# Softmax weight sums moved from TensorE, ScalarE and VectorE to DMA transposes and GpSimd, in a fused attention and ReGLU kernel

## The chip, the core and the metric

The kernel runs on one core of one Trainium2 chip. The metric is the device time of one launch, in microseconds (us), as the median of several runs. Each run also lists the core's span (first to last instruction) and its mean granted TensorE clock, 1.0 being full speed (in the trace of before, an output matmul of 512 columns has a record of 0.39 us at 1.0 and of 0.61 us at 0.5). Engines: TensorE (PE; its weight loads are PEld), VectorE (DVE), ScalarE (ACT), GpSimd (POOL), SyncE (SP), which issues the DMAs. In the code, PSUM is the memory that the matmuls write, handed out in banks ("gate banks" for the gates, one "output bank"); all other tiles on the chip lie in SBUF.

## The reference

Two attention steps through 32 inducing points, then a gated feed-forward layer.

```
x: 4 x 12416 x 128      inducing: 32 x 128      scale = 1/sqrt(128)
mab(q, kv): a = softmax(scale * q @ kv.T);  return a @ kv
h   = mab(inducing, x)            # 4 x 32 x 128
y   = mab(x, h)                   # 4 x 12416 x 128, flattened to 49664 rows
out = (relu(y @ w_gate) * (y @ w_val)) @ w_out      # d_ff = 1536, fp32 out
```

Each row's softmax weights have to be divided by their sum. Gate and value are both linear in the weights, and ReLU passes a positive factor through, so the kernel leaves the 32 weights p2 of a row undivided and multiplies the output row twice by 1/sum at the end. The sum itself ("weight sum", z2) is what the change moves.

## The kernel before

x of one batch is cut into 24 blocks of 512 rows and a rest of 128. Since `y @ w_gate` is `p2 @ (h @ w_gate)`, the kernel forms `hgv = h @ [w_gate | w_val]` once per batch, and gate and value come from matmuls with 32 contraction rows. A unit is one slice of 128 hidden columns for two blocks: four such matmuls, one ReLU of each gate bank on ScalarE, and one product gate x value on VectorE. There are 588 units in all, 147 a batch.

```
    # PSUM: "g" three banks (gates and everything small), "v" two double banks, "o" one bank
    def bank(tag, name, ...): bufs={"g": 3, "v": 2, "o": 1}[tag]
    ...
    # one slot of the loop: value matmuls of an older unit, gate matmuls of a new one,
    # perhaps one "fill" (small work that takes a gate bank), two or so steps of an output chain
        g16 <- Relu(gate banks)                     # ScalarE, two of 128x512
        dst <- g16 * v                              # VectorE, 128x1024
```

The weight sums, once for four blocks, as a fill:

```
    def ev_z2(b, qd, first, last):
        def pe(at):
            ps = bank("g", "z2_ps", [P, TPB, 4])
            for t in range(TPB):
                nc.tensor.matmul(ps[:, t, :], p2qs[(b, qd)][:, cols], sel4, ...)
            ...
            def act():  nc.scalar.copy(out=z2, in_=ps)
            def dve():  nc.vector.reciprocal(out=z2i, in_=z2)
```

The weights of four blocks come out of one Exp as p2q (four row groups of 32); eight DMAs of 32 rows copy them twice each, because in this kernel the gate and the value matmuls of a unit read different rows (in the trace of before two gate and two value matmuls then start together, at 655.12 and 655.13 us):

```
        for j in range(2):
            for k in range(2):
                for d in range(2):
                    nc.sync.dma_start(
                        out=p2[j][64 * k + 32 * d : 64 * k + 32 * d + 32, :],
                        in_=p2q[64 * j + 32 * k : 64 * j + 32 * k + 32, :])
```

While a batch is worked on, h of the next one is collected in parts. The "join" adds the parts with small fp32 matmuls (two calls, four records in the trace); where it comes, near the end of a batch, is called the hand-over. It takes the only output bank, in the queue of output chains:

```
        def join():
            ps = s["hz_ps"] = bank("o", "hz_ps", [P, 2, M], FP32)
            nc.tensor.matmul(ps[:, 0, :], s["hp"][:, 0:P], stackI, ...)
            nc.tensor.matmul(ps[:, 1, :], s["zl"], stackI, ...)
        ...
        s["join"] = ([(at0 + 124, join)], finish, ([1], [1]))     # finish: VectorE makes hT
```

The softmax here doesn't subtract the row's maximum and nothing guards it: scores larger than these inputs give would overflow.

Of the kernel before, what the change touches and what calls it, by code (L numbers as in the profile page):

```python
# [10 lines left out]
FP32 = mybir.dt.float32  # L11
# [7 lines left out]
def kernel(  # L19
# [85 lines left out]
    sel2 = constp.tile([P, 2], FP16, name="sel2")  # L105
    nc.vector.memset(sel2, 0.0)
    nc.vector.memset(sel2[0:32, 0:1], 1.0)
    nc.vector.memset(sel2[64:96, 1:2], 1.0)
    sel4 = constp.tile([P, 4], FP16, name="sel4")
    nc.vector.memset(sel4, 0.0)  # L110
    for r in range(4):
        nc.vector.memset(sel4[32 * r : 32 * r + 32, r : r + 1], 1.0)
# [45 lines left out]
    def hgv_pe(hT, k, ps=None):  # L158
        if ps is None:
            ps = bank("g", "hgv_ps")  # L160
        for r in range(4):
            nc.tensor.matmul(
                ps[32 * r : 32 * r + 32, :],
                hT[:, 0:M],
                (wg if r % 2 == 0 else wv)[:, k * BLK : (k + 1) * BLK],
                start=True,
                stop=True,
            )
# [9 lines left out]
    def s2_pair_pe(hT, xT, pr):  # L178
        ps = bank("g", "s2_ps")
        for k in range(2):  # L180
            nc.tensor.matmul(
                ps[64 * k : 64 * k + 64, :],
                hT,
                xTs(xT, (2 * pr + k) * TPB, TPB),
# [28 lines left out]
    def p2_copies(p2q):  # L213

        p2 = [st([P, BLK], FP16, "p2", 4) for _ in range(2)]
        for j in range(2):
            for k in range(2):
                for d in range(2):
                    nc.sync.dma_start(
                        out=p2[j][64 * k + 32 * d : 64 * k + 32 * d + 32, :],  # L220
                        in_=p2q[64 * j + 32 * k : 64 * j + 32 * k + 32, :],
                    )
        return p2

    def s2_rest_pe(hT, xT):
        ps = bank("g", "s2_ps")
        nc.tensor.matmul(ps[0:64, 0:P], hT, xTs(xT, NT - 1, 1), start=True, stop=True)
        return ps

    def s2_rest_exp(ps):  # L230
        p2 = st([64, P], FP16, "p2r", 2)
        nc.scalar.activation(out=p2, in_=ps[0:64, 0:P], func=AF.Exp, scale=sm_scale)
        return p2
# [150 lines left out]
    def ev_s2_pair(b, pr, first, last):  # L384
        def pe(at):
# [5 lines left out]
            post[at + 1].append(act)  # L391

        fill(first, last, pe)

    def ev_s2_quad(b, qd, first, last):
        def pe(at):
# [9 lines left out]
            post[at + 2].append(copies)  # L406

        fill(first, last, pe)

    def ev_s2_rest(b, first, last):  # L410
        def pe(at):
# [5 lines left out]
            post[at + 1].append(act)  # L417

# [3 lines left out]
    def ev_z2(b, qd, first, last):  # L422
        def pe(at):
            if qd < NPAIR // 2:
                ps = bank("g", "z2_ps", [P, TPB, 4])
                for t in range(TPB):
                    cols = slice(t * P, (t + 1) * P)
                    if (b, qd) in p2qs:
                        nc.tensor.matmul(
                            ps[:, t, :], p2qs[(b, qd)][:, cols], sel4, start=True, stop=True  # L430
                        )
                    else:
                        for j in range(2):
                            nc.tensor.matmul(
                                ps[:, t, 2 * j : 2 * j + 2],
                                p2s[(b, 2 * qd + j)][:, cols],
                                sel2,
                                start=True,
                                stop=True,
                            )  # L440
            else:
                ps = bank("g", "z2_ps", [P, 1, 1])
                nc.tensor.matmul(
                    ps[:, 0, :], p2s[(b, NPAIR)], sel2[0:64, 0:1], start=True, stop=True
                )

            def act():
                n = ps.shape[1] * ps.shape[2]
                tag = "4" if n > 1 else "1"
                z2 = st(ps.shape, FP32, "z2" + tag, 2)  # L450
                nc.scalar.copy(out=z2, in_=ps)

                def dve():
                    z2i = st(ps.shape, FP32, "z2i" + tag, 3)
# [526 lines left out]
```

## Time and profile before

| | before |
|---|---|
| median of the first three runs | 730.74 us (730.72 to 734.59) |
| VectorE busy | 95% |
| ScalarE busy | 94% |
| TensorE busy | 89% |
| GpSimd busy | 30% |
| granted clock, mean of the span | 0.991 |

Two engines run at their limit side by side. The lines themselves are shown in the prediction.

### The profile page before, as it was taken

What the parts mean: (1) busy time and instruction counts of PE and PEld (TensorE: products, weight loads), DVE (VectorE), ACT (ScalarE), POOL (GpSimd) and SP (SyncE); (2) the same over time, 40 slices, a digit from 0 to 9 for tenths busy, and PEclk for the clock granted to TensorE, in tenths of its full rate; (3) what the DMA queues carried; (4) which work ended last, traced back from release to release, by engine and by line L of the source; (5) the groups of instructions that cost most, each with busy time, mean ns of one, the idle gap of its engine ahead of it and who ended that gap; (6) DMA issues with size and microseconds to landing.
All of it is one profiled execution on the core that took longest, in us unless ns stands there. A gap on an engine that the chain in (4) does not pass through costs nothing.

```text
span 729.2 us, 14099 instructions
## 1 busy us (share of the span) xinstructions
PE 652.5 (89%) x4653; PEld 195.5 (27%) x4653; DVE 689.4 (95%) x666; ACT 682.9 (94%) x1400; POOL 220.5 (30%) x440
## 2 busy tenths in 40 slices
PE   5889898998898999898988999999889898898896
PEld 5422222222222222222222222222223222222222
DVE  4599999999999999999999999999999999999996
ACT  4599999998999999999999999999999999999985
POOL 3422325322131433433122243443212221221221
PEclk9999999999999999999999999999999999999999
DMA  9546667521256776722235975852212222222122
GB/s 339 200 115 166 146 160 167 109 74 51 57 135 137 189 173 154 175 75 72 44 76 152 152 200 127 197 121 74 65 55 77 58 80 63 61 80 66 59 66 71
DMA packets 130490, 84.57 MB, mean 116 GB/s; under 512 B 104912, under 2 KB 113904, under 8 KB 128112
## 3 DMA queue, kind: packets, MB, share of 16 engines
q1 hardware_dynamic: 130416, 83.67, 45.1%
q8 instruction: 36, 0.59, 0.4%
q14 instruction: 38, 0.31, 0.1%
HBM read 27.80 MB, written 25.43 MB: 73 GB/s over the span
## 4 chain that ended last, share of the span: by engine, by line
PE 40%; ACT 23%; issue 16%; DVE 15%; DMA 5%; SPq 1%; POOL 0%; ACTq 0%; DVEq 0%
PE o_ps L657 17%; ACT g L944 17%; DVE gv L947 14%; PE v_ps L849 12%; PE g_ps L849 6%; ACT oT L663 5%; DMA gv<-in_x_dram 2%; DMA out_dram<-osb 1%; PE s1T_ps L529 1%; PE idle_ps L278 1%; DMA p<-p2q 1%; PE s_ps L199 1%; PE o_ps L713 1%; ACT p2q L210 0%; ACT hgv L172 0%
## 5 line engine op out<-in xcount | busy, mean ns | idle before, releaser
L947 DVE TENSOR_TENSOR gv<-g,v_ps 128x1024 f16<-128x1024 f16 x576 | 662.8, 1219 | 17.0 <-PE g_ps L849 7.2
L944 ACT ACTIVATE g<-g_ps 128x512 f16<-128x512 f32 x1164 | 615.5, 616 | 24.4 <-PE g_ps L849 16.5
L657 PE MATMUL o_ps<-gv,wo 128*128 128x512 f16 x1128 | 340.8, 385 | 33.2 <-ACT oT L663 31.7
L849 PE MATMUL g_ps<-p,hgv 32*128 32x512 f16 x1152 | 285.9, 382 | 7.2 <-ACT g L944 2.3
L674 POOL TENSOR_SCALAR osb<-o,z2i 128x128 f32<-128x128 f16 x380 | 164.5, 447 | 404.3 <-DMA o<-oT 248.2
L849 PE MATMUL v_ps<-p,hgv 32*128 32x512 f16 x1152 | 227.6, 386 | 10.8 <-DVE gv L947 9.1
L849 PEld LDWEIGHTS <-hgv 32*128 32x128 f16 x2400 | 73.8, 91 | 269.1 <-issue 263.1
L657 PEld LDWEIGHTS <-wo 128*128 128x128 f16 x1176 | 79.3, 97 | 188.3 <-issue 162.1
L663 ACT CAST oT<-o_ps 128x512 f16<-128x512 f32 (+1 forms) x98 | 57.4, 586 | 0.1
L508 POOL CAST x<-x 128x2048 f16<-128x2048 f32 x18 | 34.0, 1890 | 16.6 <-DMA x<-in_x_dram 12.4
L613 POOL TENSOR_TENSOR hp<-hp,hq 128x129 f32<-128x129 f32 (+1 forms) x18 | 8.2, 456 | 48.6 <-ACT hq L612 43.6
L331 DVE COPY xT<-xT_ps 128x1024 f16<-128x1024 f16 (+1 forms) x13 | 8.5, 651 | 7.0 <-PE xT_ps L330 5.7
L210 ACT ACTIVATE p2q<-s_ps 128x512 f16<-128x512 f32 x23 | 14.0, 610 | 0.0
L302 ACT ACTIVATE p<-s_ps 128x256 f16<-128x256 f32 (+2 forms) x14 | 5.0, 356 | 7.6 <-PE s_ps L300 7.6
L539 ACT ACTIVATE p1T<-s1T_ps 128x512 f16<-128x512 f32 x18 | 11.9, 662 | 0.0
L330 PE MATMUL xT_ps<-eye,x 128*128 128x128 f16 x97 | 9.2, 249 | 1.6 <-POOL x L294 0.9
L294 POOL CAST x<-gv 128x1024 f16<-128x1024 f32 x6 | 6.2, 1040 | 12.6 <-DMA gv<-in_x_dram 12.6
L199 PE MATMUL s_ps<-xT,hT 128*32 128x512 f16 x92 | 9.2, 388 | 0.7
L292 ACT CAST x<-gv 128x1024 f16<-128x1024 f32 (+1 forms) x6 | 5.8, 967 | 3.9 <-DMA gv<-in_x_dram 3.9
L947 DVE TENSOR_TENSOR gvr<-g,v_ps 128x512 f16<-128x512 f16 x12 | 8.0, 684 | 1.5 <-PE g_ps L849 1.5
L529 PE MATMUL s1T_ps<-xT,indT 128*32 128x512 f16 x72 | 7.2, 388 | 1.1
L330 PEld LDWEIGHTS <-x 128*128 128x128 f16 x97 | 6.9, 112 | 2.3 <-POOL x L294 1.1
(101 smaller groups left out, 166.5 us busy)
## 6 DMA issues: line engine op xcount, KB each, us to landing
out_dram<-osb SPq DMA_DIRECT2D x94, 256.0 KB, 2.2
x<-in_x_dram SPq DMA_DIRECT2D x18, 1024.0 KB, 5.8
p<-p2q SPq DMA_DIRECT2D x184, 32.0 KB, 1.9
gv<-in_x_dram SPq DMA_DIRECT2D x11, 512.0 KB, 8.3
o<-oT SPq DMA_TRANSPOSE x98, 2.4
x<-in_moe_w_out_dram SPq DMA_DIRECT2D x1, 768.0 KB, 9.2
gv<-in_x_dram SPq DMA_DIRECT2D x2, 256.0 KB, 9.5
x<-in_moe_w_gate_dram SPq DMA_DIRECT2D x1, 512.0 KB, 8.0
```

Of the source, the lines that this page charges most:

```text
L199: nc.tensor.matmul(ps[32 * r : 32 * r + 32, :], hT[:, 0:M], xTs(xT, (4 * qd + r) * TPB, TPB), start=True, stop=True,)
L210: nc.scalar.activation(out=p2q, in_=ps, func=AF.Exp, scale=sm_scale)
L330: nc.tensor.transpose(ps[:, t - t0, :], x16[:, t, :], eye16)
L508: nc.gpsimd.tensor_copy(out=s["x16"][:, t0:t1, :], in_=s["x32", q])
L529: nc.tensor.matmul(ps[32 * r : 32 * r + 32, :], indT, xTs(s["xT"], t, TPB), start=True, stop=True,)
L539: nc.scalar.activation(out=p1T, in_=ps, func=AF.Exp, scale=sm_scale)
L657: nc.tensor.matmul(c["ps"][:, 0:w], wo[:, i, :], gv(i), start=(i == 0), stop=(i == NFF - 1))
L663: nc.scalar.copy(out=oT[:, 0:w], in_=c["ps"][:, 0:w])
L674: nc.gpsimd.tensor_scalar(out=osb[:, t, :], in0=o16[:, t, :], scalar1=zz, scalar2=zz, op0=ALU.mult, op1=ALU.mult,)
L849: nc.tensor.matmul(ps[:, cols], hgv[:, s * P : (s + 1) * P], p2, start=True, stop=True)
L944: nc.scalar.activation(out=g16[:, k * BLK : (k + 1) * BLK], in_=ps, func=AF.Relu)
L947: nc.vector.tensor_tensor(out=ready["dst"], in0=ready["g16"][:, 0:n], in1=ready["v"][:, 0:n], op=ALU.mult)
```

## The change

Its intent: take the weight sums off the three busy engines. p2q is transposed by DMA, so that a row's 32 weights lie along the free dimension; GpSimd adds them in five halvings and raises the sum to the power -1. Besides, the row order becomes gate, gate, value, value, so that two copies lie together and four DMAs of 64 rows do the work of eight; the join goes to the gate banks as a fill; three output rings (sets of buffers used in turn) get a fourth buffer.

```
-        for k in range(2):  for d in range(2):   # eight copies of 32 rows
+            for d in range(2):
+                nc.sync.dma_start(out=p2[j][64 * d : 64 * d + 64, :], in_=p2q[64 * j : 64 * j + 64, :])
... (rows of the matmul operands follow: gate 0 to 63, value 64 to 127)
-    def ev_z2(b, qd, first, last):          # matmuls, ScalarE copy, VectorE reciprocal
+    def ev_z2(p2, keys, n, at):
+        def tr():
+            nc.sync.dma_start_transpose(out=p2T, in_=p2()[0:rows, :])
+            def add():
+                m = M // 2
+                while m:
+                    nc.gpsimd.tensor_tensor(out=dst, in0=v[:, :, :, 0:m], in1=v[:, :, :, m:2*m], op=ALU.add)
+                    v, m = dst, m // 2
+                def power():
+                    nc.gpsimd.tensor_tensor(out=z2i, in0=v[:, :, :, 0], in1=minus1, op=ALU.pow)
+                post[at + 7].append(power)
+            post[at + 5].append(add)
+        post[at].append(tr)
...
-            ps = s["hz_ps"] = bank("o", "hz_ps", [P, 2, M], FP32)
+            ps = s["hz_ps"] = bank("g", "hz_ps", [P, 2, M], FP32)
-        s["join"] = ([(at0 + 124, join)], finish, ([1], [1]))
+        fill(at0 + 120, at0 + 124, join, True)
...
-            oT = st([P, BLK], FP16, "oT", 3)          # o16 and osb alike
+            oT = st([P, BLK], FP16, "oT", 4)
```

More of the change, by code (lines that the diff above doesn't have):

```diff
@@ L104 @@
     nc.vector.memset(ones16, 1.0)
-    sel2 = constp.tile([P, 2], FP16, name="sel2")
-    nc.vector.memset(sel2, 0.0)
-    nc.vector.memset(sel2[0:32, 0:1], 1.0)
-    nc.vector.memset(sel2[64:96, 1:2], 1.0)
-    sel4 = constp.tile([P, 4], FP16, name="sel4")
-    nc.vector.memset(sel4, 0.0)
-    for r in range(4):
-        nc.vector.memset(sel4[32 * r : 32 * r + 32, r : r + 1], 1.0)
+    minus1 = constp.tile([P, 4 * TPB], FP32, name="minus1")
+    nc.gpsimd.memset(minus1, -1.0)
     ind16 = constp.tile([M, C], FP16, name="ind16")
@@ L164, in hgv_pe @@
                 hT[:, 0:M],
-                (wg if r % 2 == 0 else wv)[:, k * BLK : (k + 1) * BLK],
+                (wg if r < 2 else wv)[:, k * BLK : (k + 1) * BLK],
                 start=True,
@@ L179, in s2_pair_pe @@
         ps = bank("g", "s2_ps")
-        for k in range(2):
+        for r in range(4):
             nc.tensor.matmul(
-                ps[64 * k : 64 * k + 64, :],
-                hT,
-                xTs(xT, (2 * pr + k) * TPB, TPB),
+                ps[32 * r : 32 * r + 32, :],
+                hT[:, 0:M],
+                xTs(xT, (2 * pr + r % 2) * TPB, TPB),
                 start=True,
@@ L216, in p2_copies @@
         for j in range(2):
-            for k in range(2):
-                for d in range(2):
-                    nc.sync.dma_start(
-                        out=p2[j][64 * k + 32 * d : 64 * k + 32 * d + 32, :],
-                        in_=p2q[64 * j + 32 * k : 64 * j + 32 * k + 32, :],
-                    )
+            for d in range(2):
+                nc.sync.dma_start(
+                    out=p2[j][64 * d : 64 * d + 64, :], in_=p2q[64 * j : 64 * j + 64, :]
+                )
         return p2
@@ L226, in s2_rest_pe @@
         ps = bank("g", "s2_ps")
-        nc.tensor.matmul(ps[0:64, 0:P], hT, xTs(xT, NT - 1, 1), start=True, stop=True)
+        for d in range(2):
+            nc.tensor.matmul(
+                ps[64 * d : 64 * d + 64, 0:P], hT, xTs(xT, NT - 1, 1), start=True, stop=True
+            )
         return ps
     def s2_rest_exp(ps):
-        p2 = st([64, P], FP16, "p2r", 2)
-        nc.scalar.activation(out=p2, in_=ps[0:64, 0:P], func=AF.Exp, scale=sm_scale)
+        p2 = st([P, P], FP16, "p2r", 2)
+        nc.scalar.activation(out=p2, in_=ps[:, 0:P], func=AF.Exp, scale=sm_scale)
         return p2
@@ L391, in pe @@
             post[at + 1].append(act)
+            ev_z2(lambda: p2s[(b, pr)], [(b, pr, k) for k in range(2)], TPB, at + 2)
         fill(first, last, pe)
@@ L406, in pe @@
             post[at + 2].append(copies)
+            keys = [(b, 2 * qd + j, k) for j in range(2) for k in range(2)]
+            ev_z2(lambda: p2qs[(b, qd)], keys, TPB, at + 7)
         fill(first, last, pe)
@@ L417, in pe @@
             post[at + 1].append(act)
+            ev_z2(lambda: p2s[(b, NPAIR)], [(b, NPAIR, 0)], 1, at + 3)
         fill(first, last, pe)
-    def ev_z2(b, qd, first, last):
-        def pe(at):
-            if qd < NPAIR // 2:
-                ps = bank("g", "z2_ps", [P, TPB, 4])
-                for t in range(TPB):
-                    cols = slice(t * P, (t + 1) * P)
-                    if (b, qd) in p2qs:
-                        nc.tensor.matmul(
-                            ps[:, t, :], p2qs[(b, qd)][:, cols], sel4, start=True, stop=True
-                        )
-                    else:
-                        for j in range(2):
-                            nc.tensor.matmul(
-                                ps[:, t, 2 * j : 2 * j + 2],
-                                p2s[(b, 2 * qd + j)][:, cols],
-                                sel2,
-                                start=True,
-                                stop=True,
-                            )
-            else:
-                ps = bank("g", "z2_ps", [P, 1, 1])
-                nc.tensor.matmul(
-                    ps[:, 0, :], p2s[(b, NPAIR)], sel2[0:64, 0:1], start=True, stop=True
-                )
-            def act():
-                n = ps.shape[1] * ps.shape[2]
-                tag = "4" if n > 1 else "1"
-                z2 = st(ps.shape, FP32, "z2" + tag, 2)
-                nc.scalar.copy(out=z2, in_=ps)
-                def dve():
-                    z2i = st(ps.shape, FP32, "z2i" + tag, 3)
-                    nc.vector.reciprocal(out=z2i, in_=z2)
-                    if n > 1:
-                        for j in range(2):
-                            z2is[(b, 2 * qd + j)] = z2i[:, :, 2 * j : 2 * j + 2]
-                    else:
-                        z2is[(b, NPAIR)] = z2i
-                post[at + 2].append(dve)
-            post[at + 1].append(act)
-        fill(first, last, pe, True)
@@ new lines, in ev_z2 @@
+    def ev_z2(p2, keys, n, at):
+        g = len(keys)
+        rows = P if g == 4 else 2 * M
+        def tr():
+            p2T = st([P, n, rows], FP16, "p2T%d" % g, 2)
+            nc.sync.dma_start_transpose(out=p2T, in_=p2()[0:rows, :])
+            def add():
+                v = p2T.rearrange("p n (g m) -> p n g m", m=M)[:, :, 0:g, :]
+                m = M // 2
+                while m:
+                    dst = st([P, n, g, m], FP32, "zt%d%d" % (g, m), 1)
+                    nc.gpsimd.tensor_tensor(
+                        out=dst, in0=v[:, :, :, 0:m], in1=v[:, :, :, m : 2 * m], op=ALU.add
+                    )
+                    v, m = dst, m // 2
+                def power():
+                    z2i = st([P, n, g], FP32, "z2i%d" % g, 3)
+                    nc.gpsimd.tensor_tensor(
+                        out=z2i,
+                        in0=v[:, :, :, 0],
+                        in1=minus1[:, 0 : n * g].rearrange("p (n g) -> p n g", n=n),
+                        op=ALU.pow,
+                    )
+                    for i, key in enumerate(keys):
+                        z2is[key] = z2i[:, :, i : i + 1]
+                post[at + 7].append(power)
+            post[at + 5].append(add)
+        post[at].append(tr)
@@ L484 @@
                 ev_s2_pair(b, 1, 5, 8)
-            ev_z2(b, qd, base + (0 if base else 10), base + (8 if base else 15))
+                ev_z2(lambda: p2s[(0, 0)], [(0, 0, k) for k in range(2)], TPB, 2)
         a = slot(b, NPAIR, 0)
         ev_s2_rest(b, a - 11, a - 4)
-        ev_z2(b, NPAIR // 2, a - 1, a + 6)
     def plan_phase1(b):
@@ L626, in h_part, with join @@
             post[at + 1].append(act)
-        def join():
-            ps = s["hz_ps"] = bank("o", "hz_ps", [P, 2, M], FP32)
+        def join(at):
+            ps = s["hz_ps"] = bank("g", "hz_ps", [P, 2, M], FP32)
             nc.tensor.matmul(ps[:, 0, :], s["hp"][:, 0:P], stackI, start=True, stop=True)
             nc.tensor.matmul(ps[:, 1, :], s["zl"], stackI, start=True, stop=True)
+            post[at + 1].append(lambda: finish(at + 1))
         def finish(at):
@@ L661, in evac @@
         def evac(at):
-            oT = st([P, BLK], FP16, "oT", 3)
+            oT = st([P, BLK], FP16, "oT", 4)
             nc.scalar.copy(out=oT[:, 0:w], in_=c["ps"][:, 0:w])
             def tr():
-                o16 = st([P, TPB, P], FP16, "o16", 3)
+                o16 = st([P, TPB, P], FP16, "o16", 4)
                 nc.sync.dma_start_transpose(out=o16[:, 0:nt, :], in_=oT[:, 0:w])
                 def scale():
-                    osb = st([P, TPB, P], FP32, "osb", 3)
-                    z = z2is[key]
+                    osb = st([P, TPB, P], FP32, "osb", 4)
+                    z = z2is[key + (k,)]
                     for t in range(nt):
-                        zz = z[:, t, k : k + 1]
+                        zz = z[:, t, :]
                         nc.gpsimd.tensor_scalar(
@@ L715, in evac @@
         def evac(at):
-            z = z2is[key][:, :, k]
+            z = z2is[key + (k,)][:, :, 0]
             zz = st([P, TPB], FP32, "zz", 2)
             nc.vector.tensor_tensor(out=zz, in0=z, in1=z, op=ALU.mult)
-            oT = st([P, BLK], FP16, "oT", 3)
-            osb = st([P, TPB, P], FP32, "osb", 3)
+            oT = st([P, BLK], FP16, "oT", 4)
+            osb = st([P, TPB, P], FP32, "osb", 4)
             for a in (0, h):
@@ L788, in units @@
                                 ]
-                                for r in (64 * k, 64 * k + 32)
+                                for r in (32 * k, 64 + 32 * k)
                             ],
@@ L807, in units @@
                         )
-                        if b + 1 < B and (pr, k) == (9, 0):
-                            job(*state[b + 1]["join"])
                     for s in range(NFF):
@@ L821, in units @@
                                     )
-                                    for k, r in ((0, 32 * j), (1, 64 + 32 * j))
+                                    for k, r in ((0, 64 * j), (1, 64 * j + 32))
                                 ]
@@ L842, in units @@
                                 ]
-                                for r in (0, 32)
+                                for r in (0, 64)
                             ],
```

## The prediction

> **What bounds the kernel now.** I read the page's busy shares first, then busy time by stretches, then VectorE's (DVE's) instructions in order of time. The first line is the busy share of each engine over the span. The other two are stretches of 100 us, with columns for busy time and instruction count of each engine, granted clock, DMA share and GB/s.
>
> ```profile
> PE 652.5 (89%) x4653; PEld 195.5 (27%) x4653; DVE 689.4 (95%) x666; ACT 682.9 (94%) x1400; POOL 220.5 (30%) x440
> ...
> 500.00:600.00 100.00, 89.34 (x602) 26.27 (x599) 97.84 (x93) 96.83 (x198) 24.49 (x57) 1.00 0.23 67
> 600.00:700.00 100.00, 88.84 (x556) 24.08 (x555) 100.00 (x93) 98.49 (x199) 25.64 (x60) 1.00 0.23 65
> ```
>
> The reader is to see two engines at their limit at once. In the last batch (600 to 700 us), which carries no preparation of a next batch, VectorE is busy 100.00 of 100 us, so every nanosecond taken from it shortens the run one for one. Before that VectorE idles about 2 us in 100 and ScalarE (ACT) 2 to 4, each waiting on the other through the gate banks. TensorE (89%) and GpSimd (POOL, 30%) have room. Now VectorE's timeline in the last batch: start, duration, instruction, count.
>
> ```profile
> 612.91 0.26 DVE L455 RECIPROCAL z2i<-z 128x16 f32<-128x16 f32 x1
> 613.07 27.19 DVE L947 TENSOR_TENSOR gv<-g,v_ps 128x1024 f16<-128x1024 f16 x24
> 640.15 0.27 DVE L455 RECIPROCAL z2i<-z 128x16 f32<-128x16 f32 x1
> 640.31 27.20 DVE L947 TENSOR_TENSOR gv<-g,v_ps 128x1024 f16<-128x1024 f16 x24
> ```
>
> Twenty-four products start between 613.07 and 640.15, so one costs 27.08 / 24 = 1.128 us of the engine. That is less than its own 1.219 us, because the next one starts before the last has ended. One reciprocal costs 613.07 - 612.91 = 0.16 us here, not the 0.25 us of its record. I price by starts, not durations, throughout.
>
> [...] between 60 and 716 us, 106 products that lie at least 80% beside GpSimd work average 1.217 us, and 289 beside none average 1.220. [...] The trace has 128x129 adds of 458 ns. [...] two gate and two value matmuls start within 0.01 us at 655.12 and 655.13.
>
> **The weight sums: removed.** For every four blocks there are four tiny matmuls, a ScalarE copy out of a gate bank and a VectorE reciprocal. The columns are count, then busy us and mean ns, then idle before:
>
> ```profile
> L429 PE MATMUL z_ps<-sel,p2q 128*128 128x4 f16 x92 | 5.5, 164 | 2.1
> L451 ACT COPY z<-z_ps 128x16 f32<-128x16 f32 x24 | 5.2, 217 | 0.0
> L455 DVE RECIPROCAL z2i<-z 128x16 f32<-128x16 f32 x24 | 6.0, 251 | 0.0
> ```
>
> With the four small ones of the rest blocks there are 28 each. VectorE: from each reciprocal's start to the next instruction's start the records sum to 6.6 us, of which 1.3 is idle that merely follows it; so 5.2 us is certain work and 6.6 the most. In the last batch they cost 0.155 us each. ScalarE: the 28 copies by the same count are 4.1 us (0.15 each), plus 0.5 idle after. TensorE: 92 + 8 + 4 matmuls, about 5.9 us, on an engine with room. The users of the third gate bank lose 28 members, which should ease some of the 7.2 us in which products waited for a gate matmul.
>
> **The weight sums: added.** 29 transposes by DMA (23 groups of four blocks, two pairs, four rests), and on GpSimd five adds and a power for each. The adds of a group make 256, 128, 64, 32 and 16 elements per partition. [...] GpSimd goes from 220 us to about 280 to 320, near 40%, still far from a bound.
>
> **The copies of p2.** SyncE issues them; each issue takes it 0.588 us (median of 184), 110.8 us in all. Half of them go: -55 us. The added transposes at 1.2 us an issue (median of the output transposes) are +33 us. These rows are count, KB each and median us to landing:
>
> ```profile
> p<-p2q SPq DMA_DIRECT2D x184, 32.0 KB, 1.9
> o<-oT SPq DMA_TRANSPOSE x98, 2.4
> ```
>
> Nothing on the compute engines waits for either now in any amount: p2q copies appear twice among the waits, 3.5 us together, on engines with slack. So this is worth about zero. The new row order puts the gate operands on rows 0 to 63 and the value operands on 64 to 127; the four matmuls still use four different row groups, so TensorE's time should not move.
>
> **The join.** Now it takes the only output bank, and the next output chain waits until VectorE has made hT:
>
> ```profile
> 176.09 0.35 DVE L148 RECIPROCAL rz<-hz_ps 128x32 f32<-128x32 f32 x1
> 176.48 0.23 DVE L150 TENSOR_TENSOR hT<-hz_ps,rz 128x64 f16<-128x64 f32 x1
> ...
> 176.76 0.61 PE L657 MATMUL o_ps<-gv,wo 128*128 128x512 f16 x1 [0.49 <-DVE hT L150]
> 177.30 0.11 PEld L849 LDWEIGHTS <-hgv 32*128 32x128 f16 x4 [0.44 <-issue]
> 177.31 0.61 PE L849 MATMUL v_ps<-p,hgv 32*128 32x512 f16 x2
> ...
> 177.30:180.40 3.10, 3.10 (x14) 0.63 (x13) 2.74 (x4) 1.99 (x4) 1.73 (x4) 0.56 0.19 73
> ```
>
> TensorE waits 0.49 us, and its clock falls to half: matmuls take 0.61 us instead of 0.39 and the granted clock (third from the end in the stretch line) is 0.56. The second hand-over (350 us) shows the same, the third (524 us) stays at 1.00. VectorE is busy 4.42, 4.53 and 4.96 us in the 5 us from 176, 350 and 524, so a slow stretch costs some 0.5 us there and, with the catching up after it, perhaps 0.9. Moving the join to the gate banks removes the wait; two joins give at most 1.8 us. But [...] VectorE's 0.5 us for hT now holds a gate bank. I count 0.8 us. The join may also come up to four slots earlier; its input zl was written 18.7 us before the join at 175.0, so it should not wait.
>
> **The sum.** Weight sums: between the 5.2 us certain and 6.6 us possible on VectorE, less something because ScalarE, which loses only 4.1 to 4.6 us, takes over as the limit before 600 us: 5.5 us. Join 0.8 us. Copies 0. From 730.7: 724.4 us, a ratio of 0.991.
>
> **Rivals.** *ScalarE becomes the bound.* It is within 1% of VectorE until 600 us and loses less; then the gain is some 4 us (727). For it: equal busy times. Against it: in the last batch only VectorE is full. *GpSimd or the transposes become a new wait*: [...] an add blocked behind a late transpose delays the scaling and the stores behind it, and after four output buffers ScalarE itself would stop. For it: transposes of x take 4.7 us to land and DMA is 0.6 to 0.7 busy in the loading stretches. Against it: each add comes five slots (some 5.7 us) after its transpose, each power seven after that, GpSimd now idles 70%, and the change deepens three output rings to four. If it bit, 733 to 745 us. *The gate banks gain more than I count*: 28 fewer users of the third bank could remove most of the small VectorE gaps, about 1 us in 50; then 719 to 721. *Nothing moves*, since the freed time turns into waits for the same gate matmuls: 729 to 731.
>
> **Range and chances.** The sum of small, mostly certain terms gives 724.4; the first and last rivals put the upper end at 729.5, the third the lower end at 719.5. Faster by over 2% would need 14.6 us, more than VectorE's removable work and half of its 17.8 us of idle between 30 and 722 us together: 0.02. Slower by over 2% needs the GpSimd rival to bite hard: 0.03. Within 2%: 0.95.
>
> **What would show it.** Right: in 600 to 700 us VectorE still full, with products at 1.128 us start to start and no reciprocals; ScalarE and VectorE busy about 4 and 6 us less; GpSimd near 300 us with no product slower than 1.22; SyncE's issue time down; no 0.49 us wait of TensorE at the hand-overs. Wrong: outputs' casts on ScalarE waiting for a transpose (a full ring), products longer beside GpSimd, power instructions of several us, gate and value matmuls no longer starting together, or the half clock appearing in new places.

The forecast's sum came to 5.5 + 0.8 + 0 = 6.3 us, that is 724.4 us. Terms are cut from the smaller sum, that of GpSimd's added work: what led to its total of 280 to 320 us came only in part from a trace, so that total stands as the author's estimate and no more. Of a slow stretch's "perhaps 0.9" us, the traces showed 0.43 to 0.54 beforehand (VectorE busy 4.42 and 4.53 us against 4.96); the rest of it, and the 0.8 us for the join, are the author's estimates too. Two readings in their numbers, from the waits of before: ScalarE's ReLUs waited 16.5 us and VectorE's products 7.2 us for gate matmuls; and one engine did wait for a DMA, GpSimd 248.2 us for output transposes, though it was busy only 30%.

## The result, and the profile after

The changed kernel takes 721.93 us (median of 4 runs, 721.80 to 723.25) against 730.86 us (4 runs): 8.9 us less, where I had said 6.3 less, and inside the range. The ratio is 0.987 with a 95% interval of 0.984 to 0.990; ratios here are the mean time of one kernel's fast runs over that of the other's of the same rounds, so not quite the ratio of the medians quoted. On a second chip it was 721.75 us against 733.16 us, 0.986 (0.983 to 0.988).

Page and stretches of the changed kernel, for the lines shown of before:

```profile
PE 640.5 (89%) x4557; PEld 190.3 (26%) x4557; DVE 685.1 (95%) x630; ACT 679.3 (94%) x1372; POOL 342.4 (48%) x615
...
500.00:600.00 100.00, 87.98 (x575) 25.57 (x574) 98.29 (x90) 97.48 (x195) 45.45 (x89) 1.00 0.25 72
600.00:700.00 100.00, 88.72 (x559) 24.01 (x556) 98.96 (x89) 97.33 (x193) 41.00 (x83) 1.00 0.25 72
```

VectorE and ScalarE are still the two full engines; VectorE's busy time fell by 4.3 us, ScalarE's by 3.6. GpSimd went up by 122 us. The small idle of VectorE in 600 to 700 is the last batch's rest, which now begins before 700. In VectorE's timeline from 600 to 660 us the reciprocals are gone, and 54 products run without a break:

```profile
599.76 61.17 DVE L934 TENSOR_TENSOR gv<-g,v_ps 128x1024 f16<-128x1024 f16 x54
```

The price on GpSimd, in its groups by shape (count, then busy us and mean ns, then idle before):

```profile
L442 POOL TENSOR_TENSOR z2i<-zt,minus 128x16 f32<-128x16 f32 x23 | 67.0, 2912 | 1.3
L435 POOL TENSOR_TENSOR zt<-p2T 128x256 f32<-128x256 f16 x23 | 15.3, 665 | 7.1 <-DMA p2T<-p2q 7.1
L435 POOL TENSOR_TENSOR zt<-zt 128x128 f32<-128x128 f32 x23 | 10.4, 453 | 1.8
L435 POOL TENSOR_TENSOR zt<-zt 128x64 f32<-128x64 f32 x25 | 8.0, 320 | 2.0
L435 POOL TENSOR_TENSOR zt<-zt 128x32 f32<-128x32 f32 x25 | 6.0, 241 | 2.0
L435 POOL TENSOR_TENSOR zt<-zt 128x16 f32<-128x16 f32 x25 | 5.4, 215 | 2.0
```

The five adds of a group take 665 + 453 + 320 + 241 + 215 = 1894 ns, the power of 16 elements 2.91 us (1.65 us for 8, 0.56 for 1). The products did not notice: some 210 of them beside GpSimd work average 1.213 us, 205 beside none 1.213.

The hand-over, now with the join in a gate bank (start, duration, engine, operation):

```profile
172.76 0.39 PE L619 MATMUL hz_ps<-stackI,zl 128*128 128x32 f32 x2
...
172.99 0.38 PE L646 MATMUL o_ps<-gv,wo 128*128 128x512 f16 x1
...
174.12 0.35 DVE L142 RECIPROCAL rz<-hz_ps 128x32 f32<-128x32 f32 x1
...
174.50 0.23 DVE L144 TENSOR_TENSOR hT<-hz_ps,rz 128x64 f16<-128x64 f32 x1
```

The next output chain starts at 172.99, right behind the join and 1.1 us before VectorE takes up h; no wait for hT is left. And the matmuls run at 0.38 us, the full clock.

**Where the clock was.** In these traces the stretches of half clock lie on a grid of 3.41 us: in that of before they begin at 29.86, 176.63 and 350.71 us, 43 and 51 times 3.413 us apart. These are two in the profile of before, each with the window ahead of it (columns as above; the third number from the end is the granted clock):

```profile
26.44:29.86 3.42, 2.18 (x21) 0.52 (x13) 2.05 (x4) 1.51 (x4) 1.98 (x2) 1.00 0.51 213
29.86:33.27 3.41, 3.41 (x14) 0.48 (x12) 2.98 (x3) 2.59 (x6) 1.38 (x1) 0.50 0.02 5
173.21:176.63 3.42, 2.67 (x22) 1.18 (x19) 3.39 (x6) 3.30 (x9) 0.68 (x2) 1.00 0.16 32
176.63:180.04 3.41, 3.28 (x13) 0.74 (x14) 3.05 (x5) 2.09 (x5) 1.73 (x4) 0.50 0.23 83
```

And the only one inside the loop of the changed kernel:

```profile
252.95:256.36 3.41, 2.60 (x18) 0.69 (x14) 3.41 (x4) 3.41 (x9) 1.09 (x3) 1.00 0.97 237
256.36:259.77 3.41, 3.41 (x15) 0.63 (x13) 2.60 (x3) 2.32 (x6) 0.00 (x0) 0.50 0.93 236
```

In a stretch TensorE is busy with hardly a pause (3.28 to 3.41 of 3.41 us), yet VectorE and ScalarE starve: in the last one VectorE works 2.60 of 3.41 us, ScalarE 2.32. In the window ahead of it TensorE had a lull: it was busy 2.18, 2.67 and 2.60 of 3.41 us. The prediction had seen two of these stretches (at the hand-overs), not the one at the start, and it priced the two as if they came in every run.

**Where the time went.** I lined up the starts of the 588 products of both kernels, in pieces in which neither profile has a half-clock stretch. Where one of the two had, I took the second profile of the same kernel (b_again, a_again, below). Starts in us from the span's start:

```
product     4      120     200     414     430     587
before    36.85  172.70  268.30  521.25  540.90  721.12
b_again   35.95  171.79  266.23  518.04  538.94  721.91
after     36.08  170.73  265.73  514.50  533.97  713.04
a_again   36.22  170.87  264.60  514.63  534.09  713.17

  4 to 120   before 135.85  after   134.65    1.20
120 to 200   b_again 94.44  a_again  93.73    0.71
200 to 414   b_again 251.81 after   248.77    3.04
414 to 430   before  19.65  after    19.47    0.18
430 to 587   before 180.22  after   179.07    1.15
                                       sum    6.28
```

So 6.3 us of the loop's gain has nothing to do with the clock. Another 1.0 us is the very end, from the end of the last product to the end of the span (6.9 us before, 5.9 after). The rest, 1.6 us of the 8.9, is left for fewer half-clock stretches. The same starts price a stretch: a piece that holds one is 1.1 to 1.4 us longer than the same piece without (seven cases in these four profiles, with starts of more products than the table has; 1.26 us on average).

### The profile page after: what moved, and what is told of

The parts are those of the page before. It is cut to its first block, busy times and chain, and to the rows that moved or that the text cites. A ratio compares the mean times of both kernels' runs of the same rounds, so it can differ in the third digit from the quotient of the medians.

```text
span 720.2 us, 13901 instructions
## 1 busy us (share of the span) xinstructions
PE 640.5 (89%) x4557; PEld 190.3 (26%) x4557; DVE 685.1 (95%) x630; ACT 679.3 (94%) x1372; POOL 342.4 (48%) x615
## 4 chain that ended last, share of the span: by engine, by line
PE 43%; ACT 22%; issue 16%; DVE 15%; DMA 4%; SPq 0%; POOL 0%; DVEq 0%; ACTq 0%
PE o_ps L646 19%; ACT g L931 15%; DVE gv L934 15%; PE v_ps L836 14%; PE g_ps L836 7%; ACT oT L652 6%; DMA gv<-in_x_dram 2%; PE s_ps L193 1%; DMA x<-in_x_dram 1%; PE o_ps L702 1%; PE s1T_ps L517 1%; PE idle_ps L273 0%; DMA p1r<-p1T 0%; ACT p1T L527 0%; ACT hgv L166 0%
## 5 line engine op out<-in xcount | busy, mean ns | idle before, releaser
L442 POOL TENSOR_TENSOR z2i<-zt,minus 128x16 f32<-128x16 f32 (+2 forms) x29 | 72.5, 2501 | 1.5
L435 POOL TENSOR_TENSOR zt<-zt 128x128 f32<-128x128 f32 (+5 forms) x116 | 33.4, 288 | 9.1
L435 POOL TENSOR_TENSOR zt<-p2T 128x256 f32<-128x256 f16 (+2 forms) x29 | 17.0, 586 | 12.5 <-DMA p2T<-p2q 7.1
```

Source lines behind the costliest of these rows:

```text
L435: nc.gpsimd.tensor_tensor(out=dst, in0=v[:, :, :, 0:m], in1=v[:, :, :, m : 2 * m], op=ALU.add)
L442: nc.gpsimd.tensor_tensor(out=z2i, in0=v[:, :, :, 0], in1=minus1[:, 0 : n * g].rearrange("p (n g) -> p n g", n=n), op=ALU.pow,)
```

## The experiments

Theory after the result: (a) the weight sums are worth 5 to 6 us because VectorE sets the pace; (b) the rest comes from half-clock stretches, which the join's place makes likelier, and from the fourth buffer at the end. Rivals: ScalarE sets the pace; the gate banks do; the clock is chance of chip and run; the added GpSimd and DMA work costs something that hides in the sum.

Names beginning with b change the kernel before, with a the changed kernel. "Stretches" are counted for each run from its mean granted clock g and span s, n = (1 - g) x s / 1.707 us (half of the 3.413 us that the stretches inside the loop take in the traces); g is given to 0.001, so n is good to about 0.2. A stretch after the last matmul counts too, with no matmul left to slow (in that of before from 726.17 us, the last matmul ending at 724.45): in the profiles it adds 0.8 to 1.0 to n in the kernel before and its variants, and 0 to 0.7 in the changed kernel and its variants. So about 2.7 of the 3.5 before and 0.8 of the 1.2 after lie in the loop. The kernel before ran beside each set, on three chips (eleven runs each).

| kernel | median us | runs from - to | mean n | ratio to before (95%) |
|---|---|---|---|---|
| before, sets 1 / 2 / 3 | 730.3 / 733.2 / 732.5 | 728.6 - 734.9 | 3.6 | |
| b_again | 731.0 | 729.3 - 733.3 | 3.3 | 1.000 (0.996 - 1.004) |
| b_ring4 | 732.0 | 730.2 - 733.8 | 3.7 | 1.002 (0.999 - 1.004) |
| b_join_g | 730.5 | 728.9 - 733.1 | 2.9 | 0.998 (0.996 - 1.001) |
| b_fill | 729.7 | 729.0 - 730.2 | 0.6 | 0.997 (0.994 - 0.999) |
| a_again | 721.8 | 721.3 - 722.1 | 1.0 | 0.986 (0.983 - 0.988) |
| a_join_o | 728.7 | 725.7 - 735.7 | 6.9 | 0.998 (0.994 - 1.003) |
| a_pe_sums | 729.0 | 726.5 - 731.5 | 2.8 | 0.997 (0.994 - 1.000) |
| a_dve_recip | 726.6 | 725.5 - 728.1 | 1.8 | 0.993 (0.990 - 0.995) |
| a_no_sums | 721.9 | 720.9 - 723.3 | 1.2 | 0.986 (0.984 - 0.989) |
| a_ring3 | 722.5 | 720.9 - 727.1 | 1.6 | 0.988 (0.985 - 0.991) |
| a_8dma | 725.5 | 721.6 - 731.0 | 2.8 | 0.991 (0.986 - 0.995) |
| a_fill | 722.7 | 721.1 - 724.2 | 0.8 | 0.987 (0.985 - 0.989) |

All gave the right result except a_no_sums, whose result is wrong on purpose.

### b_again and a_again: both kernels unchanged, once more

> The kernel before, unchanged, for a second profile of its half-clock stretches. Theory: such a stretch of 3.4 us follows a window of low TensorE use whose place is a matter of phase, so the start (29.9 us) and the hand-overs (177, 351, 525 us) are where they can fall, but not all of them in each execution; each costs about 1.2 us. Expected: 730.7 us in most runs, others off by steps of about 1.2 us, and two to four stretches in the profile. Rival (the stretches are fixed by the program): the same three at the same places, and no spread.

Measured: 729.3 to 733.3 us; the profile has stretches at 522, 539 and 700 us and at the end, none at the start and none at the first two hand-overs. (The "low use" of the expectation is, ahead of the three stretches in the loop of before, 36 to 38% by the count below.) So the places are not fixed by the program, and the rival falls. Over the 37 runs of the kernel before (33 beside the experiments, 4 here) a straight line through time against n is 726.5 us + 1.48 us x n, with a correlation of 0.95: nearly all of its scatter is the count of half-clock stretches, 1.7 to 6.0 a run.

> The changed kernel, unchanged, for the spread of its times and its half-clock stretches. Theory (low-use windows): a free window of 3.41 us that starts in one of its lulls has the array used under about 37% and the next window runs at half clock for some 1.3 us; its lulls are 3.4 us of starts in all, so one stretch on average, against 12.3 us and 3.6 stretches before. Expected 719.5 to 724 us, median 722, at most two stretches in the profile. Rival (chance of that chip): spread as wide as the kernel before, 721 to 728 us.

Measured: 721.3 to 722.1 us, n from 0 to 1.7, one stretch inside the loop of the profile (428 us). The nine runs of the changed kernel have 1.2 stretches on average against 3.5. Its narrow spread holds on another chip, as the theory has it. With 1.48 us each, 2.3 fewer stretches are 3.4 us; with the 1.9 fewer in the loop at the 1.26 us of the product starts they are 2.4. The changed kernel's own nine runs do not confirm the higher price: a line through them is 721.4 us + 0.5 us x n (n from 0 to 2.5), and why it is so flat is not shown.

What sets them off? For every window of the grid between 24 and 722 us in six profiles (some 1200 windows) I added up the array's use. The weights are my own choice, which no trace shows: each matmul counts 0.213 us for 512 columns (in the trace, output matmuls of 512 columns in a row start 0.215 us apart at the least; with that, shares of 36% come out 0.3 points higher), four times as much in fp32 (which touches little but the joins: counted once, before's two windows at its joins come to 32 and 33% in place of 36 and 38%), times its rows / 128, times its output columns / 128, so a 32-row gate matmul counts a quarter. Of the 14 full-clock windows used under 36.5%, all 14 were followed by half clock; of the 8 between 36.5 and 37.7%, 5; of all others, none. That is a fit to six profiles (before, after, b_again, b_ring4, a_join_o, a_pe_sums). Counted the same way, the eight later profiles agree: 6 of 6 windows under 36.5% were followed by half clock, 2 of the 3 between, and one more, at 38.3%. So in these fourteen profiles the two kinds overlap between 36.5 and 38.3%, by this count. TensorE's busy share does not tell the windows apart: those before a half clock were 56 to 86% busy; one that was 82% busy was followed by half clock (b_ring4, 172.9 us), one that was 60% busy and used 41% was not (a_no_sums, 26.2 us). Two experiments put it to the test (b_fill, a_fill).

Letting the window start anywhere, one can add up for how much of a run a start would be under 36.5%: 12.3 us in the kernel before by my first count, of which 7.0 at its hand-overs, and 3.4 us in the changed one, none of it at a hand-over. Divided by 3.41, this gives an estimate of 3.6 and 1.0 stretches. A recount from the traces gives the 3.4 again, but only 8 to 10 us for the kernel before, so 2.4 to 2.9 stretches; that fits the 2.7 in its loop, while the fit of 3.6 to the 3.5 of the table, which counts the end too, was luck.

### b_fill: the kernel before, with spare matmuls in its lulls

```
+            for _ in range(3):     # behind the join, in unused columns of its bank
+                nc.tensor.matmul(full[:, 2*M:BLK], eye16, wg[:, 2*M:BLK], start=True, stop=True)
...  # in some output chains, the first step (start=True) is done twice: same result
+                if again and w == BLK:
+                    nc.tensor.matmul(c["ps"], wo[:, i, :], gv(i), start=True, stop=True)
```

> The kernel before, with the same repeats in its lulls and three spare matmuls of 448 columns after each join. Nothing else is changed: the sums, rings and join are as before. Theory: about 12 us of low-use starts become some 1 to 3 us, the stretches fall from 3 or 4 to one or none: 726 to 728 us, 3 us below the kernel before. Rival (the added matmuls only cost, and the clock falls for other reasons): 730 to 733 us.

Measured: no half-clock stretch in the loop of its profile, n 0 to 0.9 (the profile's stretch after the last matmul alone makes up its 0.9), and all six runs between 729.0 and 730.2, where the kernel before beside them spread over 729.8 to 734.4; ratio 0.997. The hand-over, as windows and in time:

```profile
173.20:176.60 3.40, 2.68 (x22) 1.20 (x21) 3.33 (x5) 2.73 (x7) 0.33 (x1) 1.00 0.38 111
176.60:180.00 3.40, 3.38 (x24) 0.91 (x22) 3.40 (x5) 3.30 (x7) 1.42 (x4) 1.00 0.01 5
```

```profile
175.63 0.39 PE L670 MATMUL o_ps<-gv,wo 128*128 128x512 f16 x1 [0.39 <-DVE hT L150]
```

The join still sits in the output bank, and TensorE still waits 0.39 us for hT, but the clock stays at 1.00 and VectorE is then busy 3.40 of 3.40 us. TensorE's busy time in the first of these windows is that of before's window at the same place (2.68 against 2.67 us), but the array's use is 51% against 36%. These two cuts are set to before's place; the grid of this run lies at 170.80, 174.21 and 177.63, and of all places where a window could lie at its three hand-overs the least used has 38%, against 30% in the kernel before. So in this run the wait alone did not bring the half clock; what differs from before is the use of the array. The time missed its expectation of 726 to 728: by the line above 0.6 stretches would give 727.4, so the added matmuls cost some 2 us themselves (1.7 by product starts).

### a_fill: the changed kernel, with nine first steps done twice

> The changed kernel, with the first matmul of nine output chains done twice (same result), in the lulls found in its trace: one more 512-column matmul lifts those windows from 33% to 39% use. Theory: almost no half-clock stretch is left, 719.5 to 720.5 us in most runs, 1 to 2 us below the changed kernel and with less spread. Rival (the stretches have another cause): the same times and stretches as the changed kernel, or 1 us more for the added work.

```
+        again = (key[1], k) == (10, 1) or (b < B-1 and (key[1], k) == (3, 0)) or (b == B-1 and ...)
+                if again and w == BLK:
+                    nc.tensor.matmul(c["ps"], wo[:, i, :], gv(i), start=True, stop=True)
```

Measured: no stretch inside the loop of its profile, as expected, but 722.7 us: the repeats give back, by product starts, about 1.1 us (0.15 to 0.22 at most of the nine places), as much as the one stretch they save. Its runs do not show fewer stretches (n 0.8, against 1.0 in a_again and 1.2 over all nine runs of the changed kernel), and the time is what the rival said. So only the one profile speaks for the theory here; in b_fill the runs do too (n 0.6, against 3.6 over the sets of the kernel before). The version is no better, and I found none that beats the changed kernel.

### a_join_o: the changed kernel, join in the output bank; b_join_g: the reverse

```
a_join_o:  the join's lines as in the kernel before (bank "o", a job between two chains)
b_join_g:  bank("g", "hz_ps", ...) and fill(at0 + 120, at0 + 124, join, True) as after
```

> The changed kernel with the join back in the output bank, as a job between two chains. Theory: the 0.5 us wait of TensorE at each of the three hand-overs comes back, and with it the half clock in one to three of them at 1.2 us each; 723.5 to 725.5 us. Rival (the join is worth nothing by itself, the clock is chance): 722 us.

Measured: 728.7 us, 3 us above the expectation, with 4.2 to 10.8 stretches a run. Its profile has six inside the loop, two in each of three batches, a whole number of windows apart:

```profile
171.35:174.76 3.41, 1.94 (x19) 0.95 (x17) 3.38 (x6) 3.19 (x7) 0.00 (x0) 1.00 0.17 38
174.76:178.18 3.42, 3.42 (x17) 0.62 (x17) 3.04 (x3) 2.17 (x4) 1.75 (x4) 0.50 0.20 77
```

The window ahead is used 29%, lower than in the kernel before (36%). That can be a matter of where the grid lies: in b_again's trace, too, a window at the worst place there would be used 30%. A line through its six runs is 719.8 us + 1.44 us x n: with no stretches this kernel would be as fast as the changed one. So the join's place is worth almost nothing by itself, and about 7 us through the clock in this setting. Joins follow each other here by 174.0 us, 51 windows, and in its profile all three have a stretch at the same place; in the changed kernel it is 172.5 and 171.3 us, 50.5 and 50.2 windows. That this is why it has so many is argued, not shown.

> The kernel before, with the join of h in the gate banks as in the changed kernel, and nothing else. Theory: the join is worth little by itself, but TensorE no longer pauses at the hand-overs, so the half-clock stretches fall from 3.5 a run to about 2 (counted from each run's granted clock), at 1.45 us each: 727.5 to 729.5 us, 2 us under the kernel before of the same chip. Rival (the stretches have nothing to do with the join): the same time and number as the kernel before. In the trace no 0.49 us wait of TensorE for hT.

Measured: 730.5 against 732.5 us, 2.9 stretches against 3.6 in the same set; no wait for hT is left in the trace. Its profile has four stretches in the loop, none at a hand-over: they lie at 192.6, 366.7, 540.7 and 701.2 us, within 1 us of those of a_pe_sums, which also has the new join and the sums on TensorE. The direction is as expected and the interval just holds 1, so for this one alone the verdict is "unclear". With 1.48 us a stretch taken off, its runs and those of before differ by 0.4 us or less.

### a_pe_sums: the weight sums back on TensorE, ScalarE and VectorE

```
-  ev_z2 with transposes, adds, power          +  ev_z2 with small matmuls, ScalarE copy, reciprocal
   (join, copies and rings stay as changed)
```

> The changed kernel with the weight sums by small matmuls, ScalarE copies and VectorE reciprocals as before; join, copies and rings stay changed. Theory: 28 reciprocals and copies come back at 5.5 us: 727.4 us (727.0 to 728.5). Rival (ScalarE is the bound in most of the run and lost only 4.1 us): 726 us. Rival (the third gate bank was the price, more than the engines' time): 729 us or more.

Measured: 729.0 us, but with 2.8 stretches. Its pieces without a stretch, by product starts against those of the changed kernel (products 4 to 130, 147 to 276, 290 to 414, 441 to 570), are 1.61 + 1.96 + 2.01 + 0.99 = 6.6 us longer. With 1.45 us a stretch taken off the means of all runs it is 724.9 against 720.2, 4.7 us. So the sums are worth 5 to 6.5 us without the clock, the whole of the loop's 6.3, and nothing is left for join, copies and row order. The 729 us of the gate-bank rival are met, but with the stretches in them. Of the sums' 4.7 to 6.6 us the reciprocals alone are 3.8 (a_dve_recip, next); how the other 1 to 3 us divide among the gate bank, ScalarE's copies and TensorE's matmuls is not separated. That the sums on TensorE also add 1.6 stretches to this kernel was not expected, and I did not look further; so the fall from 3.5 to 1.2 is the join and the sums together, and the join alone (b_join_g) is not shown to bring it.

### a_dve_recip: only the reciprocals back on VectorE

```
-                    nc.gpsimd.tensor_tensor(out=z2i, in0=v[:, :, :, 0], in1=minus1, op=ALU.pow)
+                    nc.vector.reciprocal(out=z2i, in_=v[:, :, :, 0])
```

> The changed kernel with the power on GpSimd replaced by VectorE's reciprocal of the added sums: 29 small VectorE instructions come back, nothing else. Theory (VectorE sets the pace): 29 at 0.155 to 0.19 us is 4.5 to 5 us where VectorE is full, so 725.5 to 726.5 us at the same number of half-clock stretches. Rival (ScalarE sets the pace up to 600 us, VectorE only after): 5 of 29 count, 723 us.

Measured: 726.6 us. Its profile has one stretch in the loop, as a_again's, and is 4.4 us longer, of which 0.6 had arisen before the loop; 3.8 us lie between products 4 and 587. The last batch shows the price plainly:

```profile
624.32 0.24 DVE L442 RECIPROCAL z2i<-zt 128x16 f32<-128x16 f32 x1
624.49 27.17 DVE L929 TENSOR_TENSOR gv<-g,v_ps 128x1024 f16<-128x1024 f16 x24
```

The reciprocal's record is 0.24 us, but the next product starts 0.17 us after it. 29 of them at 0.13 us (3.8 / 29) are most of what the sums cost. Of the 3.8 us, 3.2 have arisen by product 441, before the last batch. VectorE sets the pace, and the rival (ScalarE up to 600 us, 723 us in all) falls.

### a_no_sums: no weight sums at all

```
-  transposes, adds, powers                    +  a constant tile of ones in place of 1/sum
```

> The changed kernel without any weight sums (ones in their place, a wrong result on purpose): no transposes, adds or powers. Theory (what was added is hidden on GpSimd and the queue): products start at the same times as in the changed kernel outside half-clock stretches; 720 to 723 us. Rival (GpSimd's load, the added transposes or their traffic cost something): 1 us or more below the changed kernel with the stretches taken off.

Measured: 721.9 us. Products 4 to 120 take 134.64 us, against 134.65 in the changed kernel; products 200 to 414 take 248.77 us in both. 122 us of GpSimd work and 29 transposes are hidden to 0.01 us. The rival falls.

### b_ring4 and a_ring3: the fourth output buffer

```
b_ring4:  oT, o16, osb 3 -> 4 in the kernel before;   a_ring3:  4 -> 3 in the changed one
```

> The kernel before, with the three output rings (oT, o16, osb) at four buffers in place of three. Theory: at the end VectorE waits 2.83 us with the last scaling for an older store out of the osb ring, of which the change saves 1.0 us; so 729.7 us, a gain of 1.0, with VectorE's last wait at some 1.9 us and for the PE transpose. Rival (the tail is shorter because the sums come earlier, or by chance): 730.7 us and the 2.83 us wait stays.

> The changed kernel with the output rings back at three buffers. Theory: the last scaling on VectorE waits for an older store again (2.8 us in place of 1.9), the end comes about 1 us later, 722.8 us; the loop itself is the same. Rival (the fourth buffers also keep GpSimd's added work from blocking ScalarE's casts): 725 us or more, with waits of ScalarE's casts on transposes.

Measured: the last scaling on VectorE, in the profiles of b_ring4 (the kernel before, four buffers) and of a_ring3 (the changed one, three):

```profile
723.94 1.13 DVE L737 TENSOR_SCALAR osb<-oo_ps,zz 128x128 f32<-128x128 f16 x4 [1.87 <-PE oo_ps L729]
```

```profile
715.78 1.13 DVE L726 TENSOR_SCALAR osb<-oo_ps,zz 128x128 f32<-128x128 f16 x4 [2.74 <-DMA out_dram<-osb]
```

With three buffers VectorE waits 2.74 us (2.83 in the kernel before) for an older store to leave the osb ring, with four 1.87 us for the PE transpose. From the end of the last product to the end of the span it is 6.9 us (before), 6.4 (b_ring4), 6.8 (a_ring3) and 5.9 (after): 0.5 us (b_ring4 against before) to 0.9 us (after against a_ring3) for the buffer. In the times this drowns: b_ring4 is no faster than before (1.002, with 3.7 stretches), a_ring3 722.5 against 721.8 us. The wait is shown, its worth in whole runs is not. No cast of ScalarE in a_ring3 waits on a transpose, so the rival falls.

### a_8dma: eight copies again

```
-            for d in range(2):                       # four DMAs of 64 rows
+            for k in range(2):
+                for d in range(2):                   # eight of 32 rows, to the same places
```

> The changed kernel with eight copies of 32 rows per group in place of four of 64, to the same places. Theory: the copies are off the path; products start at the same times to 0.2 us, 721.8 us, only SyncE's issue time grows by 55 us. Rival (the queue is full enough that later transposes and stores slip): 723 us or more.

Measured: 725.5 us, from 721.6 (no stretch) to 731.0 (7.7 stretches). The expectation failed. Up to product 360 the profile agrees with the changed kernel's outside its stretch; then, by product 400, it loses 3.6 us. SyncE's timeline at that place, of a_8dma:

```profile
469.07 0.34 SPq L675 DMA_DIRECT2D out_dram<-osb  x1
469.50 4.97 SPq L213 DMA_DIRECT2D p<-p2q  x8
...
480.47 1.93 SPq L533 DMA_TRANSPOSE p1g<-p1T  x1
```

Of a_again, at the same place:

```profile
464.03 2.41 SPq L212 DMA_DIRECT2D p<-p2q  x4
...
473.59 2.01 SPq L531 DMA_TRANSPOSE p1g<-p1T  x1
```

Issuing eight copies holds SyncE for 4.97 us, four for 2.41. Here they begin late, after a store that had waited for GpSimd (a power, 2.91 us, and a scaling had come first), and the transposes behind them are late in turn: the one that TensorE's next part of h needs is issued at 480.47 us instead of 473.59. TensorE then stands still for 1.53 us up to 483.69 (the profile puts this down to an older ReLU; in the view by tile its weight loads wait for that transpose three times, 2.3 us in all, and never in a_again), and two half-clock stretches follow at 485.6 us. So with eight copies SyncE does not always get the 29 added transposes out in time. One profile shows the chain; the times (2.8 stretches against 1.2) fit it, and two of the six runs (721.6 and 722.2 us) lost nothing.

## Why the prediction was right, point by point

**The bound.** Right. VectorE sets the pace: giving it back only the reciprocals costs 3.8 to 4.4 us (a_dve_recip), where the prediction had 5.2 us of VectorE as certain and 6.6 as the most; its price in the last batch, 28 at 0.155 us or 4.3, was the better one.

**Weight sums, "5.5 us".** Right in mechanism and in size: 4.7 to 6.6 us for the sums alone (a_pe_sums), 6.3 by product starts for the whole change's loop. That ScalarE would "take over as the limit" did not happen.

**What was added.** The author's estimate for GpSimd, "280 to 320" us, was too small: it rose to 342 us, with 1.89 us for the adds of a group and 2.91 for its power. It made no difference: all of it is hidden (a_no_sums).

**The copies, "about zero".** Wrong as it stood. Taken from the kernel before it looked right, because hardly anything waited for copies there (3.5 us in all). With the added transposes behind them, eight copies sometimes make a transpose late (a_8dma, 725.5 us). The step counted SyncE's issue time as a total with room (-55, +33 us; 29 at 1.2 us are 35, and the trace has 36.9) and did not ask what stands behind a block of eight (in a_8dma the block took SyncE 4.97 us, and the transpose that TensorE needs was issued at 480.47 us, against 473.59 in a_again). The new row order did no harm: after the change gate and value matmuls still start together (601.02 and 601.03 us) and take 380 and 384 ns on average, against 382 and 386 before.

**The join, "I count 0.8 us".** Here the size was wrong. The prediction saw the wait and the half clock together and priced them as two stretches in fixed places, at 0.9 us or so each. The wait itself costs almost nothing (a_join_o's line starts at 719.8 us; b_fill keeps the wait and the full clock). The stretches cost 1.3 us each by product starts and 1.5 by the line through the runs, number 3.5 a run before and 1.2 after (2.7 and 0.8 in the loop), and so are worth 2.4 to 3.4 us. In these profiles one came after every window used under 36.5% by my count (20 of 20) and after none above 38.3%; the windows ahead of stretches at the join's old place were used 29% (a_join_o) and 36 and 38% (before), and stretches came elsewhere too (29.9 us in before, 700 us in b_again). That the join alone brings the number down is not shown (b_join_g is unclear); that its old place raises it in the changed kernel is (a_join_o).

**The tail.** Missing from the sum. The fourth buffer was read only as a safety for late transposes; it also takes 0.9 us off the last scaling's wait and 0.5 to 0.9 us off the end (b_ring4, a_ring3).

**The rivals.** "ScalarE becomes the bound" and "nothing moves" did not come. "GpSimd or the transposes become a new wait" did not come either, but a_8dma shows it a few microseconds away. Of the signs of being wrong two came all the same, a power of 2.91 us and a half clock at a new place (256 us); neither told of a wrong bound. "The gate banks gain more than I count" came nearest with its number, 719 to 721, but for a wrong reason: the surplus was the clock and the end, and the products' waits for a gate matmul did not fall (7.2 us before, 9.0 after).

**The sum.** 8.9 us measured, 6.3 predicted. The means of all runs differ by 9.8 us (731.7 over 37 runs of before, 721.9 over nine of after). The product starts give 6.3 of it and the end 1.0; 2.5 are left for the stretches, which fits 1.9 fewer in the loop at 1.26 us. (The line's price, 3.4 us, would leave 6.4 for the rest, which is less than those 7.3.) That the number came within the range is in part luck: the join's 0.8 us stands where 2.4 to 3.4 us of clock and 1.0 us of the end belong.

## What to carry to other kernels

When two engines are full, price a small instruction by what it delays the next start, and move it to whichever engine has room, even at ten times its cost (here a power of 2.91 us on GpSimd for a reciprocal of 0.25 us on VectorE). Before crediting a few microseconds to a change, count the half-clock stretches of every run from its mean granted clock: here each is worth 1.3 to 1.5 us, and they explain nearly all the scatter of the kernel before and a quarter to a third of the gain. Look at what stands behind a block of DMAs on one queue before calling it free: here eight copies (4.97 us of SyncE) in place of four (2.41 us) took the kernel from 721.9 to 725.5 us.
